# HGRN2 attention and MLP on one core: keys of seven late units through DRAM, VectorE in program order, the next k turned behind the states, and sums of o read by ScalarE

## Chip, cores, metric

One core of one Trainium2 chip. The metric is device time in microseconds (us) of that core for one launch.

## What is computed

A gated linear attention (HGRN2) over 4 x 8 heads, 768 tokens, head size 48, then an MLP on its output, all in fp32. Cut to what matters:

```python
f = 1.0 / (1.0 + np.exp(-f_logit))
for t in range(S):                         # S = 768
    state = f[:, :, t, :, None] * state + np.einsum('bhd,bhe->bhde', k[:, :, t], v[:, :, t])
    y[:, :, t] = np.einsum('bhd,bhde->bhe', q[:, :, t], state)
x = y.transpose(0, 2, 1, 3).reshape(3072, 384)
h = x @ w_in                               # 384 x 2048
g = h * (1.0 / (1.0 + np.exp(-1.702 * h)))
out = g @ w_out                            # 2048 x 384
```

## The kernel before

The 3072 tokens are cut into 12 units of 256. TensorE runs in the order of the program. Between the parts of a unit's attention its stream is filled with the MLP of an earlier unit: 16 columns `h` (6 matmul records each), then `o` by a scheme of seven products over four sums (o_X, o_W, o_Y, o_Z). A function decides after each part how much fill follows, from a table of shares. All other engines are ordered by a scheduler.

The parts that matter here: the scores work on q and k with the head dimension on the partitions (`X`), while the state products need k with the tokens on the partitions (`kn`). So the keys have to be turned once more, after they were multiplied by their gates level by level:

```python
def turn_k(a0):
    if a0 == 0:
        t["kn"] = att.tile([P, NP, NG, P], F32, tag="kn", name=f"kn_{n}", bufs=1)
    pt = ps.tile([P, 2, NG, P], F32, tag="mm", name=f"tkn_{n}_{a0}", bufs=4)
    for a in range(2):
        for g in range(NG):
            x = (a0 + a) * U + g * G
            nc.tensor.transpose(pt[:, a, g, :], X[:, 1, x:x + G], ident)   # 8 per unit
    nc.scalar.copy(t["kn"][:, a0:a0 + 2], pt)

for a0 in (0, 2):
    part("T")(lambda a0=a0: turn_k(a0))

@part("S")
def _():                                   # state products, 64 per unit
    if n >= N_FILL:
        adds(NL - 2, 0)                    # y products of the last levels
    adds(NL - 1, 0 if n < N_FILL else 256)
    pd = scores()
    # ... loops over a, g, h, c:
    nc.tensor.matmul(
        pd[h * HS:(h + 1) * HS, c, x:x + D],
        lhsT=t["kn"][c * C:(c + 1) * C, a, g, h * HS:(h + 1) * HS],
        rhs=vns[n][c * C:(c + 1) * C, g, (2 * a + h) * D:(2 * a + h + 1) * D],
        start=True, stop=True,
    )
    # ... the states on VectorE
```

What the next unit needs is begun inside this one: `begin_f` (gates), `begin` (q), `begin_k` (k).

```python
def turn(j, out, fn=None):                 # late units
    nc.vector.transpose(...)               # 128x1024, about 2 us
    ...
def begin():
    turn(1, X[:, J, 1:])
    q_last[n] = att.tile([P, NP], F32, tag="q_last", name=f"q_last_{n}", bufs=2)
    nc.gpsimd.tensor_copy(q_last[n], view(X, J * NX + U, [[U, NP]]))
    nc.gpsimd.tensor_copy(view(X, J * NX, [[U, NP]]), q_last[n - 1])
def begin_k():
    turn(2, X[:, 1, :NA])
    if n >= N_FILL:
        set_aside(0, True)                 # ScalarE copies Kc and Qc of 128x512
        promote(0)                         # VectorE product X <- X, gates
```

The order of the parts in a late unit, and two of the sums of `o`:

```python
kind, states = parts.pop()
parts += [("B", begin_k), (kind, lambda: (states(), begin_gates()))]
parts.insert(i - 3, ("B", lambda: (begin_f(), begin())))
...
def p6():
    nc.vector.tensor_tensor(row("u2"), t["p1"], t["Y"], ALU.add)   # o_Y goes on after this
def p3():
    nc.vector.tensor_tensor(out_(0)[:, HC:], t["u2"], t["Z"], ALU.add)
```

## Time and profile before

| | before |
|---|---|
| time | 656.39 us (656.24 to 657.39, 3 runs) |
| span of the profiled run, clock | 653.7 us, 1.00 |
| TensorE busy | 632.3 us, 97% |
| TensorE waits for keys in late units | none |
| length of a late unit, from one start of the state products to the next | 48.7 us |

The prediction shows the lines of this profile.

### The profile page before, as it was taken

Reading aid. Unit: us, or ns where it says so; the run is one execution under the profiler, and the core shown is the slowest. Engines: PE = TensorE matmul, PEld = TensorE weight load, DVE = VectorE, ACT = ScalarE, POOL = GpSimd, SP = SyncE. Lnnn points to the kernel's source line nnn. Section 1 sums busy time; section 2 is a strip of 40 time slices with the busy share of each in tenths; the row PEclk is TensorE's granted clock in tenths of the full one; section 3 lists DMA queues with packets and bytes.
Section 4 is the critical chain, followed back from the end, with each engine's and each line's share of the span. In section 5 each row is a group of like instructions: output and inputs, shape, how many; then the busy total and the mean of one; then the engine's idle time right before and its main releaser. Section 6 shows DMA issues by size and latency. Waiting matters only on the chain.

```text
span 653.7 us, 20397 instructions
## 1 busy us (share of the span) xinstructions
PE 632.3 (97%) x8958; PEld 542.0 (83%) x8958; DVE 444.7 (68%) x802; ACT 229.7 (35%) x477; POOL 60.2 (9%) x116
## 2 busy tenths in 40 slices
PE   6979989999999999999999999999999999999997
PEld 5656767767778789989989989989989889989997
DVE  2998978788787658558558558558559557553571
ACT  3565444333224324324324324324334333232120
POOL 3050020010001002002002002002002002000000
PEclk9999999999999999999999999999999999999999
DMA  8898874384044634614605615605604202101000
GB/s 186 211 221 216 216 157 126 99 207 79 25 91 123 167 74 121 164 29 119 167 25 127 160 27 128 159 26 129 159 27 107 64 25 64 38 2 26 25 1 24
DMA packets 67554, 67.67 MB, mean 104 GB/s; under 512 B 30410, under 2 KB 61290, under 8 KB 67466
## 3 DMA queue, kind: packets, MB, share of 16 engines
q1 hardware_dynamic: 67466, 66.38, 40.5%
q8 instruction: 70, 1.15, 0.7%
q14 instruction: 18, 0.15, 0.1%
HBM read 56.92 MB, written 8.65 MB: 100 GB/s over the span
## 4 chain that ended last, share of the span: by engine, by line
PE 85%; DVE 8%; DMA 3%; ACT 2%; issue 1%; SPq 1%; DVEq 0%; ACTq 0%
PE h L727 37%; PE o_X L704 7%; PE o L755 7%; PE o_Y L704 7%; PE o_Z L704 7%; PE sc L384 5%; PE y L448 4%; PE o_W L704 4%; PE t L339 2%; PE y L563 2%; PE sc L523 1%; PE tkn L505 1%; DMA bits<-in_moe_w_in_dram 1%; DMA xT<-yT 1%; DVE X L439 1%
## 5 line engine op out<-in xcount | busy, mean ns | idle before, releaser
L727 PE MATMUL h<-xT,w_in 128*128 128x256 f32 (+1 forms) x1152 | 259.8, 381 | 5.7 <-DMA xT<-yT 3.0
L727 PEld LDWEIGHTS h<-xT,w_in 128*128 128x128 f32 x1152 | 215.3, 190 | 39.1 <-issue 3.8
L733 DVE TENSOR_TENSOR g<-h,sg 128x256 f32<-128x256 f32 (+1 forms) x192 | 80.8, 422 | 98.2 <-ACT sg L732 95.7
L732 ACT ACTIVATE sg<-h 128x256 f32<-128x256 f32 (+1 forms) x192 | 73.2, 383 | 193.1 <-PE h L727 186.9
L423 ACT COPY Kc<-X 128x512 f32<-128x512 f32 x69 | 46.2, 669 | 118.1 <-DVE X L439 84.7
L755 PE MATMUL o<-w_out,g 128*128 128x384 f32 x192 | 66.1, 493 | 0.0
L439 DVE TENSOR_TENSOR X<-X,tot 128x1024 f32<-128x1024 f32 x45 | 55.1, 1224 | 15.4 <-PE sc L384 10.2
L755 PEld LDWEIGHTS o<-w_out,g 128*128 128x128 f32 x192 | 35.3, 190 | 22.9 <-issue 1.4
L704 PE MATMUL o_X<-w_out,g 128*128 128x192 f32 x288 | 51.9, 329 | 0.0
L704 PE MATMUL o_Y<-T,S 128*128 128x192 f32 x288 | 51.1, 331 | 0.1
L704 PEld LDWEIGHTS o_Y<-T,S 128*128 128x128 f32 x288 | 46.5, 190 | 2.6 <-DVE u L679 1.2
L704 PEld LDWEIGHTS o_X<-w_out,g 128*128 128x128 f32 x288 | 47.3, 190 | 0.9
L410 DVE TENSOR_TENSOR A<-sc,masks 128x512 f32<-128x512 f32 x72 | 46.8, 679 | 0.0
L376 POOL TENSOR_TENSOR tot<-F 128x512 f32<-128x512 f32 x12 | 12.5, 1040 | 342.2 <-DVE st L540 342.2
L448 PE MATMUL y<-A,vl 64*48 64x64 f32 x2304 | 41.2, 217 | 0.4 <-issue 0.3
L448 PEld LDWEIGHTS y<-A,vl 64*48 64x48 f32 x2304 | 36.2, 120 | 3.9 <-issue 3.6
L327 DVE STREAM_TRANSPOSE X<-raw 128x1024 f32<-128x1024 f32 x18 | 36.7, 2040 | 2.5 <-PE y L563 2.2
L571 ACT COPY yT<-y 48x512 f32<-48x512 f32 x48 | 27.8, 580 | 13.0 <-PE y L563 12.4
L384 PEld LDWEIGHTS sc<-X,Kc 48*64 48x64 f32 x1344 | 24.0, 134 | 8.2 <-issue 3.4
L384 PE MATMUL sc<-X,Kc 48*64 48x64 f32 x1344 | 28.3, 220 | 1.8 <-DVE A L410 1.0
L376 POOL TENSOR_TENSOR tot<-tot 128x256 f32<-128x256 f32 (+4 forms) x60 | 27.4, 457 | 4.7
L704 PE MATMUL o_Z<-w_out,g 128*128 128x192 f32 x144 | 26.6, 331 | 0.0
(93 smaller groups left out, 662.5 us busy)
## 6 DMA issues: line engine op xcount, KB each, us to landing
vl<-v_tok SPq DMA_DIRECT2D x60, 192.0 KB, 2.9
bits<-in_moe_w_out_dram SPq DMA_DIRECT2D x8, 768.0 KB, 10.4
bits<-in_moe_w_in_dram SPq DMA_DIRECT2D x8, 576.0 KB, 7.0
v_tok<-in_v_dram SPq DMA_DIRECT2D x10, 384.0 KB, 4.2
vn<-v_tok SPq DMA_DIRECT2D x10, 384.0 KB, 6.9
xT<-yT SPq DMA_DIRECT2D x24, 144.0 KB, 2.8
raw<-in_q_dram SPq DMA_DIRECT2D x18, 192.0 KB, 4.0
raw<-in_f_logit_dram SPq DMA_DIRECT2D x18, 192.0 KB, 4.8
```

The source lines that it names most:

```text
L327: nc.vector.transpose(out.rearrange("p (a i j) -> p a j i", a=NP, j=R), raw[:, j].rearrange("p a (j d) -> p (a j) d", j=R)[:, :, :32],)
L376: nc.gpsimd.tensor_tensor(tn, t2[:, :, 0], t2[:, :, 1], ALU.mult)
L384: nc.tensor.matmul(out[g * HS:(g + 1) * HS, h, a, :], lhsT=lhs(h, a * U + g * G), rhs=rhs(h, a * U + g * G), start=True, stop=True,)
L410: nc.vector.tensor_tensor(A[:, :, c:c + w].rearrange("p h (x t) -> p h x t", t=64), t["sc"][:, :, c:c + w].rearrange("p h (x t) -> p h x t ...
L423: nc.scalar.copy(c.rearrange("p (n m) -> p n m", m=m), X[:, j, :NA].rearrange("p (n two m) -> p n two m", two=2, m=m)[:, :, hf, :],)
L439: nc.vector.tensor_tensor(qk, qk, by, ALU.mult)
L448: nc.tensor.matmul(dst(h, g, a), lhsT=vls[n, u][g * 64:(g + 1) * 64, (2 * a + h) * D:(2 * a + h + 1) * D], rhs=A(h, g, a), start=(start an ...
L704: nc.tensor.matmul(t[bank], lhsT=lhs(f), rhs=rhs(f), start=(new and f == 0), stop=(f == HF - 1), skip_group_check=True,)
L727: nc.tensor.matmul(ph, lhsT=w_in[:, c, ff * P:(ff + 1) * P], rhs=xTs[n][:, c, :], start=(c == 0), stop=(c == NK - 1))
L732: nc.scalar.activation(sg, ph, AF.Sigmoid, scale=1.702)
L733: nc.vector.tensor_tensor(g[ff // FG][:, ff % FG, :], ph, sg, ALU.mult)
L755: nc.tensor.matmul(t["po"], lhsT=g[ff // FG][:, ff % FG, tt * P:(tt + 1) * P], rhs=w_out[:, ff, :], start=(ff == ffs[0]), stop=(ff == ffs[ ...
```

## The change

Its intent: take the eight key transposes of seven units out of TensorE's stream. VectorE turns 32x32 blocks of the keys, four DMAs write them to DRAM, a fifth reads them back with the tokens on the partitions, and ScalarE copies them into `kn`. To keep this in step VectorE runs in program order, the shares of fill get a table of their own, the next k is turned after the states, and the sum o_Y, which TensorE goes on with, is read by ScalarE alone. Cut to its core:

```diff
+    CARRY = range(N_FILL + 1, NALL - 1)              # units 4 to 10
-    ctx.enter_context(tc.manual_schedule(engines={mybir.EngineType.PE}))
+    ctx.enter_context(tc.manual_schedule(engines={mybir.EngineType.PE, mybir.EngineType.DVE}))
+    k_toks = [tc.dram_tile([NG, G, P // 32, 32 * NP], F32, name=f"k_tok{j}") for j in range(2)]
+        def carry_k(g):
+            nb = G // 32
+            z = mlp.tile([P, nb, 32, NP], F32, tag="sum", name=f"z_{n}_{g}", bufs=3)
+            nc.vector.transpose(
+                z.rearrange("p b d a -> p a b d"),
+                X[:, 1, :NA].rearrange("p (a g b t) -> p g a b t", a=NP, g=NG, b=nb)[:, g],
+            )
+            for i in range(P // 32):
+                nc.sync.dma_start(
+                    out=k_toks[n % 2][g, :, i].rearrange("(b t) x -> t b x", t=32),
+                    in_=z[i * 32:(i + 1) * 32].rearrange("p b d a -> p b (d a)"),
+                )
+        def fetch_k(g):
+            if g == 0:
+                t["kn"] = att.tile([P, NP, NG, P], F32, tag="kn", name=f"kn_{n}", bufs=1)
+            z = mlp.tile([P, P, NP], F32, tag="sum", name=f"kt_{n}_{g}", bufs=3)
+            nc.sync.dma_start(out=z.rearrange("p d a -> p (d a)"), in_=k_toks[n % 2][g].rearrange("t i x -> t (i x)"))
+            nc.scalar.copy(t["kn"][:, :, g, :], z.rearrange("p d a -> p a d"))
-        for a0 in (0, 2):
-            part("T")(lambda a0=a0: turn_k(a0))
+        if n not in CARRY:
+            for a0 in (0, 2):
+                part("T")(lambda a0=a0: turn_k(a0))
+        else:
+            parts[-1] = "V3", parts[-1][1]
+            part("C")(lambda: (carry_k(0), fetch_k(0)))
+            part("C2")(lambda: (carry_k(1), fetch_k(1)))
@@ sums of o
-            nc.vector.tensor_tensor(row("u2"), t["p1"], t["Y"], ALU.add)
+            nc.scalar.copy(row("p6"), t["Y"])
-            nc.vector.tensor_tensor(out_(0)[:, HC:], t["u2"], t["Z"], ALU.add)
+            nc.vector.tensor_tensor(out_(0)[:, HC:], t["p1"], t["Z"], ALU.add)
+            nc.vector.tensor_tensor(out_(0)[:, HC:], out_(0)[:, HC:], t["p6"], ALU.add)
@@ order of the parts
-                parts += [("B", begin_k), (kind, lambda: (states(), begin_gates()))]
-                parts.insert(i - 3, ("B", lambda: (begin_f(), begin())))
+                parts += [("S1", lambda: (states(), begin_gates())), ("K3", begin_k)]
+                parts.insert(5 if n in CARRY else i - 3, ("B", begin_f))
+                parts.insert(6 if n in CARRY else i - 1, ("B", begin))
@@ shares of fill in units 4 and later (cut: small additions to two other tables)
+    def late(kind):
+        return {"V": 6, "V3": 2, "C": 2, "C2": 4, "S1": 3, "S": 5, "B": 3, "K3": 5, "T": 2, "W": 5}.get(kind, 0)
-        merge(n, fill, NFF * NK * U + 7 * HF * HC, steady, chores=list(sums_of_b()) if n == 4 else ())
+        merge(n, fill, NFF * NK * U + 7 * HF * HC, late, chores=list(sums_of_b()) if n == 4 else ())
```

More of the change, by code (lines that the diff above doesn't have):

```diff
@@ L853, in merge @@
         total = sum(share(kind) for kind, _ in parts)
-        converting = {"W": 3, "T": 3, "B": 1} if n < N_FILL - 1 else {"W": 3, "V": 4, "S": 3, "T": 1, "B": 1}
+        converting = {"W": 3, "T": 3, "B": 1} if n < N_FILL - 1 else {"W": 3, "V": 4, "S": 3, "T": 1, "B": 1, "K3": 3}
         total_ops = sum(converting.get(kind, 0) for kind, _ in parts)
@@ L881, in steady @@
     def steady(kind):
-        return {"W": 3, "V": 4, "S": 3, "T": 1, "B": 1, "K": 1}.get(kind, 0)
+        return {"W": 3, "V": 4, "S": 3, "T": 1, "B": 1, "K": 1, "S1": 1, "K3": 3}.get(kind, 0)
+    def late(kind):
+        return {"V": 6, "V3": 2, "C": 2, "C2": 4, "S1": 3, "S": 5, "B": 3, "K3": 5, "T": 2, "W": 5}.get(kind, 0)
     UNIT = NFF * NK * U + U // P * NFF * DM
```

## The prediction

> **What bounds the kernel now.** I read the page first (busy shares, then the chain that ended last, then the costliest groups):
>
> ```profile
> PE 632.3 (97%) x8958; PEld 542.0 (83%) x8958; DVE 444.7 (68%) x802; ACT 229.7 (35%) x477; POOL 60.2 (9%) x116
> ...
> PE 85%; DVE 8%; DMA 3%; ACT 2%; issue 1%; SPq 1%; DVEq 0%; ACTq 0%
> ...
> L327 DVE STREAM_TRANSPOSE X<-raw 128x1024 f32<-128x1024 f32 x18 | 36.7, 2040 | 2.5 <-PE y L563 2.2
> ...
> vl<-v_tok SPq DMA_DIRECT2D x60, 192.0 KB, 2.9
> ```
>
> TensorE is busy 97% and carries 85% of the chain, so only what TensorE does, or waits for, counts. The windows of whole units tell in which stage (columns: length, then PE, PEld, DVE, ACT, POOL busy, clock, DMA share, GB/s):
>
> ```profile
> 0.00:125.00 125.00, 110.74 (x1929) 81.61 (x1930) 97.73 (x223) 55.85 (x108) 19.92 (x44) 1.00 0.75 182
> 125.00:255.00 130.00, 126.37 (x1567) 97.42 (x1566) 99.30 (x170) 43.83 (x91) 9.76 (x19) 1.00 0.45 110
> ...
> 403.75:452.50 48.75, 48.75 (x732) 44.67 (x736) 32.73 (x53) 17.25 (x37) 4.83 (x9) 1.00 0.40 105
> ```
>
> A late unit takes 48.75 us and TensorE has no gap in it. TensorE's idle time, 14.3 + 3.6 us, lies before 255 us, where weights are converted; the change hardly touches that part. So in the late units the gain is what leaves TensorE's stream. The TensorE timeline of one unit (start, length, instruction) gives its price:
>
> ```profile
> 437.61 0.60 PE L505 MATMUL tkn<-ident,X 128*128 128x128 f32 x4
> 438.05 2.76 PE L727 MATMUL h<-xT,w_in 128*128 128x256 f32 x12
> 440.64 0.60 PE L505 MATMUL tkn<-ident,X 128*128 128x128 f32 x4
> 441.08 1.46 PE L727 MATMUL h<-xT,w_in 128*128 128x256 f32 x6
> ...
> 454.40 2.87 PE L704 MATMUL o_Y<-T,S 128*128 128x192 f32 x16
> 457.11 2.76 PE L704 MATMUL o_Z<-T,g 128*128 128x192 f32 x16
> 459.71 2.86 PE L704 MATMUL o_Y<-T,S 128*128 128x192 f32 x16
> ```
>
> Four key transposes push the next matmul back by 438.05 - 437.61 = 0.44 us, 0.11 us each; their printed durations (0.27 us) overlap. The o_Y groups are 0.1 us longer than o_Z of the same shape, which the waits of TensorE's weight loads in the late units explain in part:
>
> ```profile
> PEld o_Y L704 <- DVE u L679: 1.2, 4, 0.3
> ```
>
> The sum that goes on (o_Y) may not be resumed before VectorE has read it.
>
> **What the Trainium skill says.** (1) "TensorE: Matmul & The Clock Gate", Part 4, gives about 275 ns for a transpose in a kernel's context and says that the result lands in PSUM and needs a copy. The trace agrees with the duration (273 ns median), but the cost to the stream is 0.11 us, which I use. (2) "VectorE: DVE Perf Modes", The three transpose paths: VectorE transposes 32x32 blocks only. Hence the trip through DRAM, which puts the blocks in place. (3) "DMA: Bandwidth & Descriptors", Two DMAs through the same engine are not ordered: a read of what another DMA wrote has to wait for the write's semaphore before it is issued. The listing of the new program does that on SP, so SP stands still there. (4) "SBUF — State Buffer", Who interferes with whom: a VectorE instruction with two SBUF inputs contends with a GpSimd instruction that reads SBUF, one with at most one does not. The trace agrees: the same GpSimd copy takes 1.04 us beside the product L439 and 0.19 us at another place:
>
> ```profile
> 455.74 1.04 POOL L357 COPY q_last<-X 128x4 f32<-128x4 f32 x1 [3.04 <-DVE X L327]
> ...
> 504.34 0.19 POOL L357 COPY q_last<-X 128x4 f32<-128x4 f32 x1 [3.04 <-DVE X L327]
> ```
>
> **Part 1, keys through DRAM.** Removed: 8 transposes in each of seven units (4 to 10), 7 x 8 x 0.11 = **6.2 us** of TensorE, all on the path. Also two ScalarE evictions of 0.58 us per unit. Added on VectorE: two transposes of half the width of L327's 2.04 us, so about 1.02 us each, 2.05 us per unit: VectorE goes from 32.7 to 34.8 us of a 48 us unit, not a bound. On ScalarE two copies of 128x512 from SBUF, about 0.67 us each as its other such copies. DMA: 0.5 MB written and 0.5 MB read per unit, about 7.3 MB in all beside 67 MB at a share of 0.40: room enough. Latency is what matters. Per half: the transpose, four issues on SP of about 0.45 us, landing of the writes about 2 us later, a read of 256 KB (2.9 us, as v_tok to vl), a copy of 0.67 us: about 9 us.
>
> **Part 2, VectorE in program order, and the next k behind the states.** The listing of the new program has in each late unit: h_4, first key transpose, h_6, second one, h_9, turn of F, h_12, turn of q, h_14, the y products, then the state products that need both halves of the keys, then h_15. A column of h takes 1.295 us, so h_6 to h_14 is 10.4 us: the second half is in time by itself, with about 1 us to spare. Before, the scheduler could turn q early, in idle time; now q is turned after h_12, and ScalarE's listing puts the copy of the q half (Qc) before the copy of the second key half. I count from the end of h_3 = 0. A g product starts 0.46 us after its h ends. VectorE is free for F at about 8.65; F 2.05, two g 0.84, two sums 1.38, one g 0.42, q 2.03 make about 15.3. The GpSimd copies take about 0.5 us (the g products beside them read PSUM and one SBUF operand), then Qc 0.6 and the key copy 0.67: **17.1**. TensorE, h_14 at 14.25 and y 1.03, wants the keys at **15.3**. On paper a new wait of up to 1.8 us in a unit. I take half of that, 0.9 us, for the terms are estimates and the uneven shares of fill look as if they were chosen to close just such waits. 7 x 0.9 = +6.3 us at the half; 0 to +13 us as the range.
>
> The k path behind the states: states 3.1, g 0.42, two sums 1.38, turn 2.03, product 1.22, copy 0.7 make 8.9 us after the state products; TensorE has h_15 1.3, o_X and o_W 7.8, y 1.0 = 10.1 us there. Hidden.
>
> **Part 3, sums read by ScalarE.** Nine copies of about 0.31 us more on ScalarE (35% busy), the adds on VectorE equal in number. ScalarE is behind two Qc/Kc copies then, done about 2.6 us after the scores and thus before o_Y is resumed at 5.2 us. It takes away 0.2 to 0.3 us per unit from o_Y over nine units: **-2 us**.
>
> The early part: turning k behind the states takes a 2.0 us turn out of VectorE's way while TensorE waits for states (138.9 to 141.3 us); worth 0 to 2 us, I take -1.
>
> **Sum.** -6.2 - 2 - 1 + half the possible wait (6.3, of which I expect tuning to have left a little less, 4) = about -5: 656.4 - 5 = **651 us**.
>
> **Rivals.** (A) The keys arrive in time: no new wait, -9 us, **647.5 us**. For it: the shares of fill between the parts are uneven in a way that looks chosen so, and 10.4 us against 9 us for the trip. (B) The new wait is whole: TensorE stands before the state products for 1.8 us or more in seven units, +13 - 9, **660 us**, and with slow landings (raw k took 5.2 us in the page, v_tok to vn 6.9) 3 us a unit, 669 us. For it: my count above, and a ScalarE queue that is in order. Against it: VectorE has 14 us of slack in a unit. (C) VectorE in order becomes the bound: a wait of one g for another holds h's PSUM buffers back. h may run four buffers ahead, 3.9 us, and no sum above delays a g by more than 2 us; I give it little, about +3 us.
>
> **Range and chances.** A and B lie 13 us apart, and the truth should lie between or at one of them: 644 to 664. Faster than 643.3 (2%) would need more than A and the early part give: 0.07. Slower than 669.5 needs 3 us a unit of new waiting: 0.06. Within 2%: 0.87.
>
> **What would show it.** Right: no transposes of the keys in units 4 to 10 and 56 fewer matmuls; a late unit of about 48 us; no wait of o_Y for VectorE. Step "half a wait" is judged by the idle time of TensorE at the state products, put down to ScalarE's kn copy: none is rival A, 1.8 us or more in each of seven units is B. The ScalarE wait just before it should be of Qc for GpSimd or VectorE (the q turn) or of kn for the DMA, and tells which link is late. If h shows waits for VectorE's g, it is C. A gain over 10 us would mean that the stream held waits which I took for work.

## The result

| | before | after |
|---|---|---|
| time, median | 656.32 us (654.54 to 657.39, 4 runs) | 675.97 us (672.15, 675.54, 676.41, 679.63) |
| ratio | | 1.0302 (95%: 1.0240 to 1.0363), slower |
| profiled span, clock | 653.7, 1.000 | 670.4, 0.987 |
| mean late unit | 48.69 us | 50.79 us |

The change costs 3%. Its page has these three lines for those shown of before (busy times; the granted clock over the span; the chain that ended last, by engine):

```profile
PE 633.5 (95%) x8902; PEld 542.3 (81%) x8902; DVE 458.3 (68%) x816; ACT 238.0 (35%) x486; POOL 53.6 (8%) x116
PEclk9999999989999999999998998998999999999999
issue 46%; PE 36%; DVE 9%; POOL 4%; ACT 3%; DMA 1%; SPq 0%; POOLq 0%; DVEq 0%; ACTq 0%
```

The 56 matmuls are gone (8958 to 8902), yet TensorE is busy for as long as before and idle for 15 us more. The second line shows slices at 8, where the clock was cut. The third line is one to distrust: 46% "issue" does not mean that nothing was waited for. The chain follows a late key copy back through ScalarE's queue into GpSimd, which is hardly used, and counts its empty time. So I turned to the waits of TensorE within 240 to 560 us, the late units. There was no such line before; now one line holds nearly all of the lost time (total, times, longest):

```profile
PE sc L552 <- ACT kn L530: 14.9, 7, 3.3
```

TensorE stands before the state products of each of the seven carrying units, for 14.9 us in all, because ScalarE has not yet copied the second half of the keys. Here is one of them on TensorE's timeline:

```profile
298.94 1.11 PE L450 MATMUL y<-A,vl 64*48 64x64 f32 x64
299.87 0.28 PE L552 MATMUL sc<-vn,kn 64*64 64x48 f32 x8
302.00 1.03 PE L552 MATMUL sc<-vn,kn 64*64 64x48 f32 x56 [1.85 <-ACT kn L530]
302.97 1.56 PE L757 MATMUL h<-xT,w_in 128*128 128x256 f32 x6
```

Eight records run on the first half of the keys, then TensorE waits 1.85 us. Why is the copy late? Follow it back over three engines, first ScalarE, then GpSimd, then VectorE:

```profile
299.05 0.38 ACT L762 ACTIVATE sg<-h 128x256 f32<-128x256 f32 x1 [0.91 <-PE h L757]
300.31 0.65 ACT L425 COPY Qc<-X 128x512 f32<-128x512 f32 x1 [0.88 <-POOL X L360]
300.87 1.08 ACT L530 COPY kn<-kt 128x512 f32<-128x512 f32 x1
```

```profile
299.84 0.19 POOL L359 COPY q_last<-X 128x4 f32<-128x4 f32 x1 [40.89 <-DVE X L329]
300.09 0.19 POOL L360 COPY X<-q_last 128x4 f32<-128x4 f32 x1
```

```profile
297.39 0.42 DVE L763 TENSOR_TENSOR g<-h,sg 128x256 f32<-128x256 f32 x1
297.73 2.05 DVE L329 STREAM_TRANSPOSE X<-raw 128x1024 f32<-128x1024 f32 x1
```

ScalarE's queue is in order, and in it the copy Qc of the next unit stands ahead of the key copy. Qc needs the q turn (ends 299.78), then two small GpSimd copies. ScalarE stands idle for 0.88 us with the key copy behind it, then takes 0.65 for Qc and 1.08 for the keys. Counted as in the prediction, from the end of h_3 (about 284.7), the q turn ends at 15.1 and TensorE resumes at 17.3. The prediction had 15.3 and 17.1.

There is a second loss that no instruction list shows. Columns of the windows: length, PE, PEld, DVE, ACT and POOL busy, clock, DMA share, GB/s. Two units of the kernel after:

```profile
302.00:351.70 49.70, 47.84 (x720) 43.95 (x721) 34.57 (x53) 18.38 (x37) 3.84 (x8) 1.00 0.49 124
351.70:403.14 51.44, 49.53 (x720) 45.32 (x721) 34.97 (x54) 18.57 (x37) 3.84 (x8) 0.97 0.47 120
```

TensorE did the same number of matmuls in both, but the second took 1.7 us more, at a clock of 0.97. The windows around another of the waits show it directly:

```profile
403.14:404.20 1.06, 1.06 (x57) 1.01 (x57) 0.00 (x0) 0.00 (x0) 0.00 (x0) 1.00 1.02 210
404.20:407.60 3.40, 3.40 (x9) 2.87 (x10) 2.77 (x8) 0.38 (x1) 0.90 (x1) 0.51 0.96 211
407.60:420.00 12.40, 12.40 (x192) 12.11 (x192) 7.62 (x8) 5.89 (x12) 2.75 (x6) 1.00 0.37 97
```

After the 1.91 us gap that ends at 403.14, and one more us, the clock is halved for about 3.4 us. The column h that took 1.56 us above takes 2.77 here:

```profile
404.10 2.77 PE L757 MATMUL h<-xT,w_in 128*128 128x256 f32 x6
```

Of the seven gaps four were followed by such a stretch (those of 3.31, 1.85, 1.91 and 2.29 us), three were not (1.85, 1.84 and 1.85 us). A unit with one is 1.5 to 2.1 us longer than the quiet 49.70, 6.9 us in all four, of which 0.5 us is only that two of these gaps are longer than 1.85 us.

The clock record in the trace shows more. In this run the five stretches at half clock start at 141.47, 250.70, 353.10, 404.30 and 455.50 us of the span, each 3.41 us long, and these starts are 32, 30, 15 and 15 times 3.413 us apart. In every profiled run with more than one such stretch the starts lie on such a grid of 3.413 us, and each of the seven cuts after a gap of the late units (four here, one in e5, two in e6) begins where the grid step that held the gap ends. So it matters how a gap lies on the grid. Two gaps of 1.85 us that no cut follows are split by a grid line, into 1.74 and 0.11 us (the one that ends at 302.00) and into 0.39 and 1.46 us (at 555.95); the gap of 1.85 us that ends at 351.70 lies in one step, and a cut follows. That is not the whole rule: the gap that ends at 506.26, 1.84 us long, lies in one step too, and no cut follows.

The lost clock also accounts for most of the scatter among the runs. If each span is reduced by (1 - clock) times itself, the four times become 663.4, 665.4, 664.3 and 662.7 us; they lie 2.7 us apart instead of 7.5. The stable part of the loss is then near 656.3 + 14.9 (waits) - 7.4 (what leaves TensorE's stream, below) = 663.8, and the rest is clock.

### The profile page after: what moved, and what is told of

It is laid out like the page before. It is cut to its first block, busy times and chain, and to the rows that moved or that the text cites. A ratio compares the mean times of both kernels' runs of the same rounds, so it can differ in the third digit from the quotient of the medians.

```text
span 670.4 us, 20447 instructions
## 1 busy us (share of the span) xinstructions
PE 633.5 (95%) x8902; PEld 542.3 (81%) x8902; DVE 458.3 (68%) x816; ACT 238.0 (35%) x486; POOL 53.6 (8%) x116
## 4 chain that ended last, share of the span: by engine, by line
issue 46%; PE 36%; DVE 9%; POOL 4%; ACT 3%; DMA 1%; SPq 0%; POOLq 0%; DVEq 0%; ACTq 0%
PE h L757 13%; PE o L785 6%; POOL tot L378 4%; PE o_Y L734 2%; PE o_X L734 2%; PE o_Z L734 2%; PE sc L552 2%; PE t L341 2%; PE sc L386 2%; DVE st L569 1%; PE y L450 1%; DVE st L572 1%; PE o_W L734 1%; ACT kn L530 1%; DMA xT<-yT 1%
## 5 line engine op out<-in xcount | busy, mean ns | idle before, releaser
L757 PE MATMUL h<-xT,w_in 128*128 128x256 f32 (+1 forms) x1152 | 263.0, 386 | 4.5 <-DMA xT<-yT 2.4
L757 PEld LDWEIGHTS h<-xT,w_in 128*128 128x128 f32 x1152 | 218.5, 192 | 38.9 <-issue 3.2
L785 PE MATMUL o<-w_out,g 128*128 128x384 f32 x192 | 67.9, 503 | 0.0
L734 PEld LDWEIGHTS o_X<-w_out,g 128*128 128x128 f32 x288 | 49.2, 196 | 0.9
L359 POOL COPY q_last<-X 128x4 f32<-128x4 f32 x12 | 2.7, 225 | 416.8 <-DVE X L329 344.9
L552 PE MATMUL sc<-vn,kn 64*64 64x48 f32 x768 | 16.0, 227 | 15.6 <-ACT kn L530 14.9
```

Of the source, the lines that this page charges most:

```text
L734: nc.tensor.matmul(t[bank], lhsT=lhs(f), rhs=rhs(f), start=(new and f == 0), stop=(f == HF - 1), skip_group_check=True,)
L757: nc.tensor.matmul(ph, lhsT=w_in[:, c, ff * P:(ff + 1) * P], rhs=xTs[n][:, c, :], start=(c == 0), stop=(c == NK - 1))
L785: nc.tensor.matmul(t["po"], lhsT=g[ff // FG][:, ff % FG, tt * P:(tt + 1) * P], rhs=w_out[:, ff, :], start=(ff == ffs[0]), stop=(ff == ffs[ ...
```

## Experiments

My theory after the result: (1) the seven waits come from the order of work (the q turn, Qc, then the key copy), since VectorE in program order can no longer turn q early; (2) the clock adds to each wait; (3) the gain on TensorE is as counted. Rivals: program order on VectorE costs by itself, whatever carries the keys; the DMA trip is too slow; the copies on ScalarE are too long. Ten kernels were run; all gave correct results. Lines of code shift by a few between kernels, so L550, L552 and L554 are the same state products.

### e1: everything but the keys

```diff
-    CARRY = range(N_FILL + 1, NALL - 1)
+    CARRY = range(0)
```

> The changed kernel with no unit's keys sent through DRAM (all by TensorE again); VectorE in program order, the k turn behind the states and ScalarE's sums stay. Theory (the whole loss is the wait of the state products for the second half of the keys, plus the lower granted clock after it): that wait is gone, clock 1.00, 652 to 658 us. Rival (VectorE in program order costs by itself): late units stay over 49.5 us, total above 662 us.

Measured: 657.69 us, ratio 0.9996 (0.9963 to 1.0029). No wait for keys, and a late unit is back at 48.5 us with a clock of 1.00 (one of the six took 49.9, with a stop of TensorE of 1.10 us for which the profile names no releaser):

```profile
299.17:347.70 48.53, 48.53 (x743) 44.66 (x737) 32.62 (x53) 17.23 (x37) 3.18 (x8) 1.00 0.42 103
```

So program order, the turned k and the sums cost nothing together. The loss needs the carried keys. The sums are in this kernel and a late unit is only 0.2 us shorter for it; e7 looks at that alone.

### e2: the keys, but VectorE left to the scheduler

```diff
-    ctx.enter_context(tc.manual_schedule(engines={mybir.EngineType.PE, mybir.EngineType.DVE}))
+    ctx.enter_context(tc.manual_schedule(engines={mybir.EngineType.PE}))
```

> The changed kernel with VectorE's order given back to the scheduler; keys still through DRAM. The listing then has q turned early and ScalarE's copy of the q half no longer ahead of the second key copy. Theory (the queue on ScalarE is the late link): the wait before the state products falls from 1.85 us to below 0.5 us a unit, clock 1.00, 648 to 656 us. Rival (the trip through DRAM itself is late): the wait stays at 1.5 us or more with the DMA as releaser, above 665 us.

Measured: 653.49 us, ratio 0.9939 (0.9904 to 0.9974). The wait for the keys is left once, 0.97 us, in the first carrying unit; the mean late unit is 47.63 us. Together with e1 this is the main finding: neither the carried keys nor the program order cost anything alone; the loss is what they do together. The trace says why: the scheduler turns q early, so Qc no longer stands ahead of the second key copy with an unfinished q before it. The q turn on VectorE, then, 34 us later, a second key copy on ScalarE, with only a sigmoid before it, then the state products without a gap:

```profile
312.81 2.06 DVE L329 STREAM_TRANSPOSE X<-raw 128x1024 f32<-128x1024 f32 x1 [0.39 <-PE y L592]
```

```profile
346.80 0.39 ACT L762 ACTIVATE sg<-h 128x256 f32<-128x256 f32 x1 [0.91 <-PE h L757]
347.08 1.12 ACT L530 COPY kn<-kt 128x512 f32<-128x512 f32 x1
```

```profile
348.92 1.10 PE L552 MATMUL sc<-vn,kn 64*64 64x48 f32 x64
```

The scheduler moved more than q here: the next k is turned before the state products again (339.64 us), and the two turns of the keys start 4.6 us apart (333.90 and 338.49) instead of 2.6. What q alone is worth is read from e5 and e9.

### e3: no copy on ScalarE, TensorE loads its weights from the landed tile

```diff
-            nc.scalar.copy(t["kn"][:, :, g, :], z.rearrange("p d a -> p a d"))
+            t["kt", g] = z
-        lhsT=t["kn"][c * C:(c + 1) * C, a, g, h * HS:(h + 1) * HS],
+        lhsT=(t["kt", g][c * C:(c + 1) * C, h * HS:(h + 1) * HS, a] if n in CARRY
+              else t["kn"][c * C:(c + 1) * C, a, g, h * HS:(h + 1) * HS]),
```

> The changed kernel without the two key copies on ScalarE: the state products load their weights straight from the landed tile, four elements apart. VectorE order as changed. Theory: with the ScalarE link cut the wait is below 0.3 us, clock 1.00, 646 to 652 us. Rival (trip late): the wait stays, released by the DMA, above 660 us. Side risk: weight loads with a stride take longer than 0.135 us each and the state products longer than 1.0 us a unit.

Measured: 659.86 us, ratio 1.0041 (1.0009 to 1.0074). The seven waits are gone, as the theory says: what is left is one wait of 0.7 us for a DMA. The number was missed, by the side cost that the expectation names: elements lie 16 bytes apart in the landed tile. By tile of this kernel, minimum, median and maximum duration in ns, carried keys first, then keys of the other units from dense rows:

```profile
L550 PEld LDWEIGHTS sc<-vn,kt x448: 189/213/215, 249.3 to 543.9; 64*64 64x64 f32 x150
L550 PEld LDWEIGHTS sc<-vn,kn x320: 129/135/135, 37.1 to 589.9; 64*64 64x64 f32 x160
```

The 64 state products took 2.08 us where they take 1.10 with dense weights, about 1 us in each of seven units, which by itself undoes the gain:

```profile
298.18 2.08 PE L550 MATMUL sc<-vn,kt 64*64 64x48 f32 x64
```
A unit is 48.6 us long.

### e4: the wait filled with idle matmuls

```diff
             adds(NL - 1, 0 if n < N_FILL else 256)
+            if n in CARRY:
+                keep_up(3)                # 3 matmuls whose result nobody reads
             pd = scores()
```

> The changed kernel with three idle matmuls of 128x384 (about 1.95 us) in front of the state products of the seven units, so that TensorE works while it waits. Theory on the clock (the low clock of 0.98 follows from the gap of 1.85 us): the keys come as late as before, but the clock is 1.00 and the time falls by about 8 us to 664 to 669 us, with less scatter between runs. Rival (the clock drops for another reason): clock stays below 0.99 and the time at 674 us or more.

Measured: 671.28 us (669.49 to 671.34), ratio 1.0201 (1.0171 to 1.0231), so 4.7 us less than the change though TensorE does more. Above the 664 to 669 expected by 2 us, but the mechanism shows. The filler (three matmuls, six records) takes 2.20 us, the keys then are there, except in the first carrying unit, where a wait of 1.2 us is left, and the next h runs at full speed:

```profile
352.77 2.20 PE L841 MATMUL idle<-masks,ident 128*128 128x384 f32 x6
354.90 1.15 PE L554 MATMUL sc<-vn,kn 64*64 64x48 f32 x64
```

```profile
354.90:404.80 49.90, 49.90 (x727) 44.99 (x726) 34.84 (x54) 18.28 (x37) 3.83 (x8) 1.00 0.47 122
```

Units from 300 us on have a clock of 1.00 and take 50.00 us in the mean against 50.79, and the runs lie 2 us apart instead of 7.5. What is left of low clock (0.991 over the span) lies before 300 us. The Trainium skill ("TensorE: Matmul & The Clock Gate", Part 1) says that an idle window of about 3.4 us halves the clock and that about as long a busy stretch restores it. The length of the slow stretch (3.40 us above) agrees. The gaps here were shorter than such a window in every case, and still 7 of the 10 gaps of 1.84 us or more in the late units of this change, e5 and e6 were followed by one; of 18 gaps up to 1.36 us in the late units of e5, e6 and e9, none was. Before the late units shorter gaps were followed by one too: in the change, gaps of 0.68 and 1.25 us that lie 0.70 us apart end at 140.53 us, and the clock falls at 141.47.

### e5: Qc of the next unit copied by GpSimd

```diff
-                nc.scalar.copy(
+                (nc.gpsimd.tensor_copy if tag == "Qc" and l == 0 and n - 1 in CARRY else nc.scalar.copy)(
```

> The changed kernel with the copy of the next unit's q half (Qc of level 0) on GpSimd in the seven units; nothing else moved, q is still turned late. Theory (Qc, ready at 15.7 us, stands ahead of the second key copy in ScalarE's queue): the key copy starts right after the sigmoid of h_14, the wait before the state products falls from 1.85 to about 0.6 us a unit (the copy itself is 1.1 us long), the clock returns to 0.99 or more, 655 to 661 us. Rival (the key copy itself has to wait for the DMA): the wait stays at 1.5 us or more, now with the DMA as releaser on ScalarE, and the time above 668 us.

Measured: 661.46 us, ratio 1.0055 (1.0011 to 1.0099). The waits fall from 14.9 to 6.0 us: 0.36 or 0.37 in three units, 0.64, 1.02, 1.08 and 2.18 in four. So Qc ahead of the key copy is more than half of the wait. The rest has a second cause, which the group of key copies shows (busy, mean ns, then idle time before them and its releasers):

```profile
L530 ACT COPY kn<-kt 128x512 f32<-128x512 f32 x14 | 15.9, 1132 | 5.3 <-DMA kt<-k_tok 2.7 <-DMA k_tok<-z 2.5
```

ScalarE, now free early, stands 5.3 us for DMAs before its 14 key copies. Of this 2.7 us is for the read of the second half, in just those four units (0.18, 0.58, 0.15 and 1.75 us, in the order of the waits above); the rest lies before first halves, 2.18 us of it in the first carrying unit. In that unit the read explains little of the wait of 1.08 us: the sigmoid in front of the copy had waited 0.90 us for a product g. The longest of the four, first the turn on VectorE, then the copy on ScalarE:

```profile
435.97 1.10 DVE L515 STREAM_TRANSPOSE z<-X 128x512 f32<-128x512 f32 x1
```

```profile
447.52 1.10 ACT L530 COPY kn<-kt 128x512 f32<-128x512 f32 x1 [1.75 <-DMA kt<-k_tok]
```

From the end of the turn to the landed read this trip took 447.52 - 437.07 = 10.4 us; the other three took 8.5, 9.1 and 9.5 us in the same count. The prediction had about 7.3 for it (9 less the turn and the copy). So the trip is slower than I counted, and in four of seven units not in time. SP's queue shows where the time of the longest goes:

```profile
434.32 1.79 SPq L520 DMA_DIRECT2D k_tok<-z  x4
438.07 0.34 SPq L529 DMA_DIRECT2D kt<-k_tok  x1
438.52 1.99 SPq L520 DMA_DIRECT2D k_tok<-z  x4
441.75 0.32 SPq L260 DMA_DIRECT2D raw<-in_f_logit_dram  x1
442.23 0.34 SPq L529 DMA_DIRECT2D kt<-k_tok  x1
```

The second half is turned by 437.07, but its writes start at 438.52, because the read of the first half stands ahead of them on SP and is issued only when that half's writes have landed. Its own read comes behind a load of raw, which in six of the seven units is issued within 0.03 us of the end of the F turn that frees its tile. In the four units the writes start 1.05 to 1.44 us after the turn, take 1.8 to 2.0 us to issue, the read is issued 1.7 to 2.4 us after them, and ScalarE goes on 3.4 to 5.3 us after that; the prediction had nothing, 1.8, 2 and 2.9 us for these. The rival "the trip is too slow" is right to that extent; in the change itself the q turn and Qc came later still and hid it.

### e6: the keys written in runs of 32

```diff
-            z = mlp.tile([P, nb, 32, NP], F32, ...)       # and z, kt, DMAs, copy to match
+            z = mlp.tile([P, nb, NP, 32], F32, ...)
```

> The changed kernel with the keys landed in runs of 32 elements in place of single elements 16 bytes apart, so that ScalarE's copy reads runs; queue order as changed. If the stride makes the copy 1.1 us long, the copy falls to about 0.67 us and the wait from 1.85 to about 1.4 us; with less gap the clock may fall less often: 664 to 672 us. If the length is due to something else: copy 1.1 us, wait and time unchanged, 672 to 679 us.

Measured: 667.14 us, ratio 1.0158 (1.0114 to 1.0202), as expected. This changes how ScalarE's copy reads: elements 16 bytes apart in the change, runs of 32 here. It also changes how VectorE's turn writes, 0.70 us in place of 1.11 (mean of 14 each), so the second half sets out earlier too; but the key copy still follows Qc at once in six of the seven units. The copies of the change, then those of e6:

```profile
L530 ACT COPY kn<-kt 128x512 f32<-128x512 f32 x14 | 15.6, 1113 | 2.4 <-DMA k_tok<-z 2.4
```

```profile
L530 ACT COPY kn<-kt 128x512 f32<-128x512 f32 x14 | 8.6, 612 | 2.7 <-DMA k_tok<-z 2.0 <-DMA kt<-k_tok 0.7
```

The copy is shorter by 0.50 us, and the wait by the same: 1.35 us in five units, 10.9 us in all with two of 2.04 and 2.10, both followed by a cut clock. (0.65 us of the 2.10 is ScalarE standing for the read.) So the copy is on the path at its full length.

### e7: the kernel before with the sums alone

```diff
-            nc.vector.tensor_tensor(row("u2"), t["p1"], t["Y"], ALU.add)
+            nc.scalar.copy(row("p6"), t["Y"])             # and p3 as in the change
```

> The kernel before with the third part alone: o_Y's first sum read by ScalarE in place of VectorE. The prediction's step was minus 2 us (0.2 to 0.3 us a unit off the o_Y group): ratio about 0.997, and no wait of o_Y for VectorE. Rival (the 0.2 us is not this wait): ratio 0.999 to 1.001.

Measured: 657.63 us against 656.40, ratio 1.0000 (0.9968 to 1.0032). A late unit is 48.50 us against 48.69, so 1.3 us over seven units in the trace; the total does not resolve it: the ratio is the rival's, but its interval holds 0.997 as well. The o_Y that goes on takes 2.76 us now, as long as o_Z took before:

```profile
365.35 2.76 PE L705 MATMUL o_Y<-T,S 128*128 128x192 f32 x16
```

### e8: the best of the parts

e2 (scheduler on VectorE, carried keys, sums), and in the units that do not carry the order of parts as before:

```diff
-                parts += [("S1", lambda: (states(), begin_gates())), ("K3", begin_k)]
-                parts.insert(5 if n in CARRY else i - 3, ("B", begin_f))
-                parts.insert(6 if n in CARRY else i - 1, ("B", begin))
+                if n in CARRY:
+                    parts += [("S1", lambda: (states(), begin_gates())), ("K3", begin_k)]
+                    parts.insert(5, ("B", begin_f))
+                    parts.insert(6, ("B", begin))
+                else:
+                    parts += [("B", begin_k), (kind, lambda: (states(), begin_gates()))]
+                    parts.insert(i - 3, ("B", lambda: (begin_f(), begin())))
```

> Keys through DRAM with VectorE's order by the scheduler (as e2), and the k turn behind the states only in the seven carrying units, the units before as in the kernel before. The late units of e2 take 47.6 us against 48.7; what e2 lost before 255 us (about 3 us) should come back: 649 to 652 us, ratio about 0.990. Rival (the early loss has another cause): as e2, 653 us or more.

Measured: 650.09 us (649.68 to 651.97, 6 runs), ratio 0.9900 (0.9874 to 0.9925): 1% faster than before. A late unit, and the one wait for keys that is left:

```profile
343.94:391.57 47.63, 47.63 (x735) 43.86 (x728) 34.73 (x55) 18.18 (x37) 4.71 (x8) 1.00 0.50 130
```

```profile
PE sc L552 <- ACT kn L530: 0.6, 1, 0.6
```

The unit is 1.06 us shorter than before, with no gap. In e2 the second half of the first carrying unit's state products starts at 253.74 us of the span, here at 248.76, after the same matmuls: the order of the parts in the units that do not carry (k turned behind the states, F and q in parts of their own, other shares of fill) cost about 5 us of the early part under the scheduler. Which of these it was is not shown. (The two were timed in different calls, and their ratios' intervals overlap by a little; the 5 us are from one profiled run of each, the medians lie 3.4 us apart.)

### e9: program order kept, q turned one part earlier

```diff
-                parts.insert(5 if n in CARRY else i - 3, ("B", begin_f))
-                parts.insert(6 if n in CARRY else i - 1, ("B", begin))
+                parts.insert(5 if n in CARRY else i - 3, ("B", (lambda: (begin(), begin_f())) if n in CARRY else begin_f))
+                parts.insert(6 if n in CARRY else i - 1, ("B", (lambda: None) if n in CARRY else begin))
```

> The changed kernel, VectorE still in program order, with the turn of q written one part earlier (before that of F, right after h_9; an empty part keeps the fill where it was). ScalarE's listing then has the q half's copy before the sigmoid of h_12 and the second key copy right after the sigmoid of h_14. Theory (what costs is where the program puts the q turn, not program order as such): the wait at the state products is 0.3 to 0.7 us a unit, late units 48.0 to 48.4 us, 654 to 659 us, as with the q copy on GpSimd. Rival (program order on VectorE is itself the cost): late units stay near 49.7 us, above 665 us.

Measured: 662.41 us, ratio 1.0083 (1.0041 to 1.0124): 3 to 8 us more than I expected. The wait is halved, to 0.87 us in each of the seven units, 6.1 us, with no cut clock there and a unit of 48.82 us. ScalarE and TensorE at one of them:

```profile
300.02 0.39 ACT L762 ACTIVATE sg<-h 128x256 f32<-128x256 f32 x1 [0.83 <-DVE g L763]
300.31 1.09 ACT L530 COPY kn<-kt 128x512 f32<-128x512 f32 x1
```

```profile
301.45 1.03 PE L552 MATMUL sc<-vn,kn 64*64 64x48 f32 x56 [0.87 <-ACT kn L530]
```

Qc is out of the way, but another link has taken its place: the gate turn now comes second, VectorE's products g come late behind it, the sigmoid sg that needs their buffer waits 0.83 us, and the key copy stands behind the sigmoid. The place of the q turn was the cause of half the wait; what was put in that place, the gates' turn with their sigmoid of 1.06 us on ScalarE, makes the other half, as far as this one timeline shows; no run took it away alone.

### e10: e8 with the layout of e6

```diff
-            z = mlp.tile([P, nb, 32, NP], F32, ...)       # and z, kt, DMAs, copy to match
+            z = mlp.tile([P, nb, NP, 32], F32, ...)
```

> The best kernel so far (keys through DRAM, VectorE by the scheduler, units before as they were) with the keys landed in runs of 32, so that ScalarE's key copies take 0.61 us in place of 1.1. Its TensorE no longer waits for these copies in the late units, so by the theory that only TensorE's stream counts this gives nothing: 649 to 651 us, ratio 0.989 to 0.991. Rival (ScalarE's load still counts): 647 us or less.

Measured: 649.54 us, ratio 0.9896 (0.9863 to 0.9928): the same as e8. The 0.5 us per copy that were worth 4.0 us of TensorE's waits in e6 are worth nothing where TensorE does not wait.

Not run: weights straight from e6's layout, so whether dense runs would save e3's slow loads is open.

## Why the prediction was wrong

Said: 651 us (644 to 664), within 2%. Measured: 675.97, slower by 3%. Term by term for the profiled run, which lies 16.7 us over the profiled run before:

| term of the sum | predicted | measured |
|---|---|---|
| key transposes | -6.2 | -6.1: 0.87 x 7 (unit 48.69 to 47.63 in e2, less the sums) |
| sums read by ScalarE | -2 | -1.3: 0.19 x 7 (e7), total unresolved |
| early part | -1 | about +0.9, counted by the matmuls done (below) |
| new wait for the keys | +4 | +14.9 |
| halved clock after the waits | not counted | +6.4 (excess of four units over the quiet 49.70, less 0.5 of longer gaps) |
| left over, in the late units and at the end | not counted | +1.9 |
| sum | -5 | +16.7 |

- **The key transposes** were right, price and count: 0.11 us each. (The 275 ns of the Trainium skill, "TensorE: Matmul & The Clock Gate", Part 4, that the prediction sets beside its 273 ns are given there for bf16; the transposes here are fp32.)
- **No bound on VectorE (rival C)**: right. No h waits for a g in the late units of the change, though VectorE is in order.
- **The k path behind the states**: right, hidden. No score waits for Kc in the late units.
- **The two GpSimd copies** beside g products: right, 0.19 us each, as the contention argument said.
- **The sums**: the wait for VectorE was real and is gone, but it was worth 0.19 us a unit over seven units; the estimate took 0.2 to 0.3 us over nine.
- **The step that failed** is this one, in the prediction's words: "On paper a new wait of up to 1.8 us in a unit. I take half of that, 0.9 us, for the terms are estimates and the uneven shares of fill look as if they were chosen to close just such waits." The count gave 17.1 us for the keys against 15.3 wanted; the trace has 17.3. It was right to 0.2 us and should have been used whole. The halving rested on a guess about the author's tuning, not on a line of the profile. Rival B, the whole wait, was what happened: 1.84 to 3.31 us in each of seven units, and the ScalarE wait just before it was that for GpSimd behind the q turn, as the prediction's last part says it would be.
- **One term within it was mis-sized**: the key copy, 0.67 us by analogy with Qc, is 1.11 us since it reads 16 bytes apart (e6: 0.61 in runs). And the trip through DRAM was counted as about 7.3 us between turn and copy and took 8.5 to 10.4 where it can be read (e5). (The steps that the prediction lists for the trip add to 8.4 us, 6.7 of it between turn and copy, not to the "about 9" it gives. It says that SP stands still for the writes, but does not count that the second half's writes then queue behind.) Together they moved the count by only 0.2 us, and for the trip that was luck: in the change the q turn (15.1 for 15.3) and Qc set the start of the copy, at 16.2 where I had 16.4, and the copy was 0.4 us longer. Rival A's argument, "10.4 us against 9 us for the trip", fell with it: without the scheduler's help the trip alone was not safely in time.
- **What was not counted at all**: rival B as written ends at 660 us. The clock after the gaps makes up about half of the way from there to 672 in the profiled run, and by their lower clocks the three other runs lost 1.4 to 8.2 us more to it.
- **The early part**: counted as a gain, in fact a loss. e1 has no late wait and yet no gain either; e2 against e8 puts about 5 us on the order in the units that don't carry, under the scheduler. In the change TensorE reaches the first state products of unit 4 3.2 us earlier than before (247.24 for 250.43 us), but has done less by then: 6 records of h, 12 of o_X and 8 key transposes, together 1.30 + 1.95 + 0.87 = 4.1 us. So 0.9 us is lost there. The h and o_X come between the state products of units 10 and 11, which lie 3.28 us further apart than before (45.95 for 42.67): moved work, no loss.
- **Two small slips** in the working changed nothing: the terms up to the q turn add to 15.37, given as 15.3, and 3.4 us of TensorE's idle time lies after 600 us, not before 255.

What stays open: what besides a gap's place on the grid decides whether the clock is cut; why the read of the keys took up to 5.3 us in e5; and the 1.9 us left over, of which about 0.2 us a unit lies beside the gap (49.70 - 1.85 = 47.85, where a unit of e2 takes 47.63).

## What to carry to other kernels

If a count of the critical path says that data comes 1.8 us too late, and each term has a row behind it, use it whole; take it apart again rather than discount it for the author's tuning. When work is moved to an engine with an in-order queue, look at what stands ahead of it there (on SP, which issues the DMAs, as well as on ScalarE), what that one waits for, and whether a fixed order elsewhere (here VectorE's) has just delayed it: each half of this change was harmless alone. And price a gap of about 2 us on TensorE at up to twice its length here, for the clock may fall for 3.4 us after it.

## What the Trainium skill lacked or had wrong

- "TensorE: Matmul & The Clock Gate", Part 1: it puts the loss of clock at an idle window of about 3.4 us; of a kernel with frequent short idles it also says that its clock oscillated, without their length. Here 7 of 10 gaps between 1.84 and 3.31 us in the late units were followed by about 3.4 us at half clock, all of them shorter than that window, and none of 18 gaps up to 1.36 us there was. Each cut began at the end of the 3.413 us grid step in which the gap, or most of it, lay. The small matmuls around these gaps (y and state products, 64x64 at most) may count as little activity; that was not tested.
- "SBUF — State Buffer", Specifications: it says that reads that cross to a new 16-byte line pay a penalty, without a figure. Here ScalarE's copy of 128x512 fp32 took 1.11 us with elements 16 bytes apart and 0.61 us in runs of 32, VectorE's turn of 128x512 took 1.11 us when it wrote at that step and 0.70 us in runs, and a weight load of 64 columns took 213 ns at that step against 135 ns dense; 64 state products went from 1.10 to 2.08 us.
- No page that I used says how long a dependent trip through DRAM takes beside other traffic: four writes of 64 KB, then one read of 256 KB that waits for them, took 8.5 to 10.4 us from the end of the turn on VectorE to the landed read in the four units of e5 where ScalarE waited for it, 1.05 to 1.44 us of it before the first write was issued.
